# One transfer for the w_in rows of heads six and seven, and s and b issued from ScalarE's queue, in a fused gated-attention and squared-ReLU kernel

## The chip, the cores and the metric

The kernel runs on one core of a Trainium2 chip. The metric is the device time of one execution in microseconds (us). Three executions of the kernel before gave 203.92, 203.97 and 204.05 us, with a median of 203.97 us. The profiled execution took 204.18 us.

## The reference

The program computes a gated linear attention for every batch and head, lays the heads side by side, and sends each token through a two-layer network with a squared ReLU:

```python
batch, n_heads, seq, head_dim = (4, 8, 768, 48)
n_tokens, d_model, d_ff = (3072, 384, 2048)

for t in range(S):
    state = alpha[:, :, t, :, None] * state + np.einsum('bhd,bhe->bhde', k[:, :, t], v[:, :, t])
    y[:, :, t] = np.einsum('bhd,bhde->bhe', q[:, :, t], state)

x = np.ascontiguousarray(attn_out.transpose(0, 2, 1, 3)).reshape(B * S, H * D)
h = x @ w_in
r = np.maximum(h, 0.0)
g = s * (r * r) + b
return (g @ w_out).astype(np.float32)
```

All inputs and the output are float32; `s` and `b` are one number each.

## The kernel before

The 3072 tokens are cut into 24 blocks of 128, six for each batch entry. Block n goes through these helpers, each named here with its engine and its line:

- `load` (L135) issues four DMAs from SyncE's queue: alpha, k, q and v of the block, each 192 KB in pieces of 192 bytes. Eight buffers of each exist.
- `ln` (L202, ScalarE) takes the logarithm of alpha; `cum` (L217 and L220, TensorE) sums it along the block, and ScalarE turns the sums into the decay factors at L228, L229 and L231.
- `qk` (L245 and L246, VectorE) scales k and q, `tr` (L251, TensorE, copied out by VectorE at L256) transposes them, `amat` (L266, masked at L274) makes the 128 by 128 score blocks.
- `vcast` (L206 and L210, GpSimd) casts v to bf16. Heads 0 to 5 go to `vp_sb` and heads 6 and 7 to `vz_sb`. The 48 columns of a head stand at places 0, 1, 2 of groups of four, and every fourth place is left for a part of head 6 or 7. So the eight heads of 48 fill three tiles of 128 rows, and `w_in` has to be loaded with its rows in the matching order.
- `inter` and `yp` (L282, L301, L326) make the attention output, which ScalarE copies to `xd_all` at L334; `state` (L345 to L366) carries the state on, mostly on GpSimd.
- `mm1` (L382) multiplies by `w_in`, ScalarE applies the ReLU (L390), VectorE squares (L397), and `mm2` (L411) multiplies by `w_out`.

The weights come in once. `load_w_in` (L142) is called for each half of the 2048 columns. Of each half, three transfers (L145) bring the rows of heads 0 to 5, 384 KB each to 32 partitions, and two (L148) bring the rows of heads 6 and 7, 192 KB each to 16 partitions. Every piece is 4 KB long. The weights are cast to bf16 by `cast_w_in` (L157 on ScalarE, L159 on VectorE), called `win` in the order below. `w_out` comes in four transfers and is scaled by `s` as it is cast (L163 and L171); `b` is used once, when `bias_row` makes the bias (L188).

The order of every engine is written out by hand; the framework only adds the semaphore waits. SyncE issues load(0), load(1), the two halves of `w_in`, `s`, `b`, load(2), load(3), the four parts of `w_out` and load(4) to load(7), in this order, before the blocks begin. ScalarE starts with a table load (L434). Its next instruction is `ln(0)`. The opening of the blocks is this list; `busy` (L192) are multiplications whose result nobody reads, and an engine runs its own part of the list in order:

```python
(ln, 0), (vcast, 0), (cum, 0), (qk, 0), (busy, 7), (tr, 0),
(ln, 1), (vcast, 1), (busy, 4), (cum, 1), (amat, 0), (qk, 1), (busy, 5),
(y, 0), (tr, 1), (busy, 4), (amat, 1), (busy, 6), (y, 1), (win, 0), (win, 1), (busy, 3),
(m, 0, 0), (m, 1, 0), (m, 0, 1), (m, 1, 1), (busy, 7), (win, 2), (win, 3), (ln, 2), (m, 0, 2), (cum, 2),
```

In the trace, every DMA of this kernel adds to one of eight completion semaphores. They are taken in turn in program order: the first DMA adds to the first semaphore, the ninth to the first again. From the ninth on, a DMA waits, before it is issued, until the one that used the same semaphore eight places earlier is complete.

Of the kernel before, what the change touches and what calls it, by code (L numbers as in the profile page):

```python
# [19 lines left out]
def kernel(  # L20
# [12 lines left out]
    nc = tc.nc  # L33
# [9 lines left out]
    KT = d_model // 128  # L43
# [32 lines left out]
    s_col = sb.tile([128, 1], FP32, name="s_col")  # L76
    b_col = sb.tile([128, 1], FP32, name="b_col")
# [30 lines left out]
    w_in_st = sb.tile([128, KT, d_ff], FP32, name="w_in_st")  # L108
# [14 lines left out]
    def load_a(n, eng=None):  # L123
        (eng or nc.sync).dma_start(out=al_sb[n % NLD], in_=src(alpha, n))

    def load_q(n, eng=None):
        (eng or nc.sync).dma_start(out=q_sb[n % NLD], in_=src(q, n))

    def load_k(n, eng=None):
        (eng or nc.sync).dma_start(out=k_sb[n % NLD], in_=src(k, n))  # L130

    def load_v(n, eng=None):
        (eng or nc.sync).dma_start(out=v_sb[n % NLD], in_=src(v, n))  # L133

    def load(n):  # L135
        if n < NBLK:
            load_a(n)
            load_k(n)
            load_q(n)
            load_v(n)  # L140

    def load_w_in(c0, c1):  # L142
        six = moe_w_in[0 : 96 * KT, c0:c1].rearrange("(t a b) f -> b a t f", t=KT, b=3)
        for r in range(3):
            nc.sync.dma_start(out=w_in_st[r::4, :, c0:c1], in_=six[r])  # L145
        two = moe_w_in[96 * KT :, c0:c1].rearrange("(x t a) f -> x a t f", x=2, t=KT)
        for e in range(2):
            nc.sync.dma_start(out=w_in_st[64 * e + 3 : 64 * e + 64 : 4, :, c0:c1], in_=two[e])  # L148

    def load_w_out(j0, j1):  # L150
        nc.sync.dma_start(
# [52 lines left out]
    def vcast(n):  # L204
        vs = v_sb[n % NLD]
        nc.gpsimd.tensor_copy(  # L206
            out=vp_sb[n % 3].rearrange("s h (a b) -> s h a b", b=4)[:, :, :, 0:3],
            in_=vs[:, 0:6].rearrange("s h (a b) -> s h a b", b=3),
        )
        nc.gpsimd.tensor_copy(  # L210
            out=vz_sb[n % 3].rearrange("s e t (a b) -> s e t a b", b=4)[:, :, :, :, 3],
            in_=vs[:, 6:8].rearrange("s e (t a) -> s e t a", t=3),
        )

    def cum(n):
# [218 lines left out]
    nc.scalar.preload_act_table_set("natural_log_exp_and_others")  # L434
    load(0)
    load(1)
    quarter = d_ff // 4
    load_w_in(0, 2 * quarter)
    load_w_in(2 * quarter, d_ff)
    nc.sync.dma_start(out=s_col, in_=moe_s.to_broadcast((128, 1)))  # L440
    nc.sync.dma_start(out=b_col, in_=moe_b.to_broadcast((128, 1)))
    load(2)
    load(3)
    for j in range(0, NJ, 4):
# [43 lines left out]
    for pos, what in enumerate(  # L488
# [5 lines that stand above are left out]
            (qk, 2), (m, 1, 2), (vcast, 2), (mm1, 0, 3), (tr, 2), (sq, 0, 3), (mm1, 1, 3), (ln, 3), (amat, 2), (sq, 1, 3),  # L494
            (busy, 4), (cum, 3), (busy, 3), (qk, 3), (y, 2), (vcast, 3), (busy, 2), (tr, 3), (m, 2, 0), (mm1, 2, 1),
            (amat, 3), (mm1, 2, 2), (wout, 0), (mm1, 2, 3), (sq, 2, 1), (sq, 2, 2), (sq, 2, 3), (busy, 2), (y, 3),
            (wout, 1), (o, 0, 0), (o, 1, 0), (m, 3, 0), (m, 3, 1), (wout, 2), (o, 0, 1), (o, 1, 1), (colsum, 1), (m, 3, 2),
            (m, 3, 3), (o, 2, 0), (wout, 3), (o, 2, 1), (ln, 4), (cum, 4), (colsum, 2), (o, 0, 2), (vcast, 4), (o, 1, 2), (o, 2, 2),
            (colsum, 3), (qk, 4), (o, 1, 3), (o, 2, 3), (tr, 4), (colsum, 4), (o, 0, 3), (amat, 4),
        ]  # L500
    ):
        at(0.1 * pos, *what)
# [12 lines left out]
    for n in range(4, NBLK):  # L515
        p = 8 * n
        if n > 4:
            f = min((n - 5) / 3.0, 1.0)
            c, t, a = 7.0 + 7.8 * f, 4.8 + 6.0 * f, 2.2 + 5.7 * f
# [44 lines left out]
```

## Time and profile before

| What | Value |
|---|---|
| Median of three executions | 203.97 us |
| Profiled execution | 204.18 us |
| Its span, first to last instruction | 202.4 us |
| Granted TensorE clock | 1.00 |
| TensorE matmul busy | 190.0 us (94%) |
| VectorE, ScalarE, GpSimd busy | 149.9, 105.8, 74.5 us |
| TensorE busy from 76 to 190 us | 113.71 of 114 us |
| TensorE busy from 24 to 76 us | 49.05 of 52 us |
| TensorE busy from 0 to 4 us | 0 |
| `busy` multiplications (L192) | 44, 13.57 us, none after 76 us |
| DMA read and written | 25.19 and 4.74 MB |
| DMA busy share by tenths, 0 to 70 us | 9 or more in nearly every slice after the first |

The share of an engine's busy time is an average over an opening of some 76 us, in which engines wait for one another, and a steady part in which TensorE never rests. The instructions of a queue start in order, and a DMA's row in the timeline begins when its waits are over. The landing of a DMA is the time at which its semaphore has all sixteen counts; the trace has these times too. For the first eight DMAs (alpha, k, q, v of blocks 0 and 1) they are 3.74, 5.11, 6.16, 7.19, 8.26, 9.32, 10.37 and 11.15 us, and for the five of the first half of `w_in` 12.29, 14.09, 16.01, 16.62 and 17.59 us.

### The profile page before, as it was taken

What the parts mean: (1) busy time and instruction counts of PE and PEld (TensorE: products, weight loads), DVE (VectorE), ACT (ScalarE), POOL (GpSimd) and SP (SyncE); (2) the same over time, 40 slices, a digit from 0 to 9 for tenths busy, and PEclk for the clock granted to TensorE, in tenths of its full rate; (3) what the DMA queues carried; (4) which work ended last, traced back from release to release, by engine and by line L of the source; (5) the groups of instructions that cost most, each with busy time, mean ns of one, the idle gap of its engine ahead of it and who ended that gap; (6) DMA issues with size and microseconds to landing.
All of it is one profiled execution on the core that took longest, in us unless ns stands there. A gap on an engine that the chain in (4) does not pass through costs nothing.

```text
span 202.4 us, 6402 instructions
## 1 busy us (share of the span) xinstructions
PE 190.0 (94%) x2580; PEld 147.1 (73%) x2583; DVE 149.9 (74%) x289; ACT 105.8 (52%) x210; POOL 74.5 (37%) x171
## 2 busy tenths in 40 slices
PE   1999989999989899999999999999999999999993
PEld 1455768675766787888788788878887878888871
DVE  6366687778789689999976877877876887796341
ACT  3224865383376565554655655565465555544440
POOL 8344015421530066447440524632600662362000
PEclk9999999999999999999999999999999999999999
DMA  6999999999999927958596957955996691111102
GB/s 123 197 283 325 175 193 355 300 175 188 172 189 172 134 27 134 160 126 189 104 241 127 193 118 126 198 100 98 173 215 110 97 198 40 43 39 42 40 3 78
DMA packets 112924, 30.35 MB, mean 150 GB/s; under 512 B 106991, under 2 KB 112126, under 8 KB 112894
## 3 DMA queue, kind: packets, MB, share of 16 engines
q1 hardware_dynamic: 112894, 29.94, 76.1%
q8 instruction: 20, 0.33, 0.7%
q14 instruction: 10, 0.08, 0.2%
HBM read 25.19 MB, written 4.74 MB: 148 GB/s over the span
## 4 chain that ended last, share of the span: by engine, by line
PE 75%; DVE 8%; DMA 5%; SPq 5%; ACT 3%; issue 2%; DVEq 0%; ACTq 0%
PE h_ps L382 28%; PE o_ps L411 25%; PE ct_ps L251 5%; PE y_ps L301 5%; DMA w_in_st<-in_moe_w_in_dram 3%; PE a_ps L266 3%; PE y_ps L282 3%; ACT r_sb L390 2%; PE a_ps L411 2%; PE h_ps L192 2%; DMA q_sb<-in_q_dram 2%; PE ct_ps L217 2%; DVE gt_all L397 1%; DVE qb_sb L246 1%; SPq L133 1%
## 5 line engine op out<-in xcount | busy, mean ns | idle before, releaser
L390 ACT ACTIVATE r_sb<-h_ps 128x512 bf16<-128x512 f32 x96 | 57.3, 599 | 52.0 <-PE h_ps L382 51.5
L382 PE MATMUL h_ps<-xd_all,w_in_bf 128*128 128x128 bf16 x1152 | 79.0, 219 | 0.6 <-ACT w_in_bf L157 0.3
L382 PEld LDWEIGHTS <-w_in_bf 128*128 128x128 bf16 x1152 | 70.7, 98 | 9.8 <-ACT w_in_bf L157 0.8
L397 DVE TENSOR_TENSOR gt_all<-r_sb 128x512 bf16<-128x512 bf16 x96 | 48.4, 508 | 32.5 <-ACT r_sb L390 32.3
L411 PE MATMUL o_ps<-w_out_bf,gt_all 128*128 128x384 bf16 x336 | 68.4, 327 | 0.3 <-DVE out_sb L424 0.3
L353 POOL TENSOR_TENSOR sd_sb<-t_sb,blast 48x144 bf16<-48x144 f32 x40 | 18.0, 451 | 93.8 <-DVE t_sb L347 52.8
L411 PEld LDWEIGHTS <-gt_all 128*128 128x128 bf16 x384 | 33.1, 98 | 16.4 <-issue 0.3
L228 ACT ACTIVATE bi_sb<-ct_ps 128x384 f32<-128x384 f32 x24 | 11.8, 491 | 17.6 <-PE ct_ps L217 13.7
L206 POOL CAST vp_sb<-v_sb 128x288 bf16<-128x288 f32 x24 | 14.6, 610 | 15.8 <-DMA v_sb<-in_v_dram 15.7
L256 DVE COPY qkT<-ct_ps 112x1024 bf16<-112x1024 bf16 x24 | 16.5, 688 | 5.3 <-PE ct_ps L251 5.3
L334 ACT ACTIVATE xd_all<-y_ps 128x384 bf16<-128x384 f32 x24 | 11.8, 490 | 13.0 <-PE y_ps L301 12.9
L274 DVE TENSOR_TENSOR am_a<-a_ps,mask 128x512 bf16<-128x512 f32 x24 | 16.4, 683 | 1.8 <-PE a_ps L266 1.6
L246 DVE TENSOR_TENSOR qb_sb<-q_sb,b_sb 128x384 bf16<-128x384 f32 x24 | 16.3, 678 | 0.7 <-ACT b_sb L229 0.7
L245 DVE TENSOR_TENSOR kb_sb<-k_sb,bi_sb 128x384 bf16<-128x384 f32 x24 | 13.4, 560 | 4.4 <-ACT bi_sb L228 4.4
L274 DVE TENSOR_TENSOR am_b<-a_ps,mask 128x512 bf16<-128x512 f32 x24 | 16.3, 679 | 0.0
L202 ACT ACTIVATE la_sb<-al_sb 128x384 bf16<-128x384 f32 x24 | 12.4, 515 | 4.0 <-DMA al_sb<-in_alpha_dram 4.0
L192 PE MATMUL h_ps<-mask,U_bf 128*128 128x512 bf16 x44 | 13.6, 422 | 0.8 <-ACT r_sb L390 0.6
L359 POOL TENSOR_TENSOR sd_sb<-t_sb,blast 48x48 bf16<-48x48 f32 x40 | 14.2, 354 | 0.0
L251 PEld LDWEIGHTS <-qb_sb 128*112 128x112 bf16 x96 | 8.8, 133 | 5.6 <-DVE qb_sb L246 3.3
L210 POOL CAST vz_sb<-v_sb 128x96 bf16<-128x96 f32 x24 | 12.2, 509 | 0.0
L217 PE MATMUL ct_ps<-la_sb,U_bf 128*128 128x384 bf16 x24 | 8.0, 333 | 4.4 <-ACT la_sb L202 4.4
L229 ACT ACTIVATE b_sb<-ct_ps 128x384 f32<-128x384 f32 x24 | 11.7, 486 | 0.7 <-DMA row_dr<-b_sb 0.7
(64 smaller groups left out, 202.9 us busy)
## 6 DMA issues: line engine op xcount, KB each, us to landing
al_sb<-in_alpha_dram SPq DMA_DIRECT2D x24, 192.0 KB, 3.1
k_sb<-in_k_dram SPq DMA_DIRECT2D x24, 192.0 KB, 3.7
q_sb<-in_q_dram SPq DMA_DIRECT2D x24, 192.0 KB, 5.1
v_sb<-in_v_dram SPq DMA_DIRECT2D x24, 192.0 KB, 4.8
out_dram<-out_sb SPq DMA_DIRECT2D x19, 192.0 KB, 1.9
w_out_st<-in_moe_w_out_dram SPq DMA_DIRECT2D x4, 768.0 KB
w_in_st<-in_moe_w_in_dram SPq DMA_DIRECT2D x6, 384.0 KB, 6.6
out_dram<-keep_sb SPq DMA_DIRECT2D x5, 192.0 KB
```

Source lines behind the costliest of these rows:

```text
L192: nc.tensor.matmul(out=h_ps[i % 2], lhsT=U_bf, rhs=mask4.rearrange("a p t -> a (p t)"), start=True, stop=True,)
L206: nc.gpsimd.tensor_copy(out=vp_sb[n % 3].rearrange("s h (a b) -> s h a b", b=4)[:, :, :, 0:3], in_=vs[:, 0:6].rearrange("s h (a b) -> s h ...
L246: nc.vector.tensor_tensor(out=qb_sb[n % 2][:, :, 0:48], in0=q_sb[n % NLD], in1=b_sb[n % 2], op=ALU.mult)
L251: nc.tensor.transpose(out=t_ps[0:112, x, p, :], in_=t.rearrange("a h d -> a (h d)")[:, 128 * p : 128 * p + 112], identity=ident,)
L256: nc.vector.tensor_copy(out=qkT_sb[n % 2][0:112].rearrange("a x p t -> a (x p t)"), in_=t_ps[0:112].rearrange("a x p t -> a (x p t)"),)
L274: nc.vector.tensor_tensor(out=am_sb[e][n % 2], in0=a_ps[e], in1=mask4, op=ALU.mult)
L353: nc.gpsimd.tensor_tensor(out=cols[:, 0:3, :, 0:3], in0=t1_sb[r, 0:3].rearrange("k p (a b) -> k p a b", b=3), in1=bl[r, 0:3].unsqueeze(3). ...
L359: nc.gpsimd.tensor_tensor(out=cols[:, 3:6, :, 3], in0=t1_sb[r, 3].rearrange("k (t a) -> k t a", t=3), in1=bl[r, 3:4].to_broadcast([48, 3, ...
L382: nc.tensor.matmul(out=hp[:, jj * N : (jj + 1) * N], lhsT=w_in_bf[:, kk, 128 * j : 128 * (j + 1)], rhs=xd_sb[g][:, kk, 0:N], start=(kk == ...
L390: nc.scalar.activation(out=rs, in_=hp, func=AF.Relu)
L397: nc.vector.tensor_tensor(out=gt_sb[g][:, u * 512 : (u + 1) * 512], in0=rs, in1=rs, op=ALU.mult)
L411: nc.tensor.matmul(out=op[:, 0:d_model], lhsT=gt_sb[g][:, j * N + t * C : j * N + (t + 1) * C], rhs=w_out_bf[:, j, :], start=(j == 0), sto ...
```

## The change

Three edits. The rows of `w_in` for heads 6 and 7 go to the partitions in another order, so that one transfer to 32 partitions replaces two to 16, once for each half. The cast of v for these heads reads its source in the matching order, with a step of three elements instead of one. And the two DMAs of `s` and `b` are issued from ScalarE's queue, after load(1) and before `w_in` in program order, instead of from SyncE's queue after `w_in`.

```diff
@@ load_w_in
-        two = moe_w_in[96 * KT :, c0:c1].rearrange("(x t a) f -> x a t f", x=2, t=KT)
-        for e in range(2):
-            nc.sync.dma_start(out=w_in_st[64 * e + 3 : 64 * e + 64 : 4, :, c0:c1], in_=two[e])
+        two = moe_w_in[96 * KT :, c0:c1].rearrange("(i t) f -> i t f", t=KT)
+        nc.sync.dma_start(out=w_in_st[3::4, :, c0:c1], in_=two)
@@ vcast
             out=vz_sb[n % 3].rearrange("s e t (a b) -> s e t a b", b=4)[:, :, :, :, 3],
-            in_=vs[:, 6:8].rearrange("s e (t a) -> s e t a", t=3),
+            in_=vs[:, 6:8].rearrange("s e (a t) -> s e t a", t=3),
@@ the opening
     nc.scalar.preload_act_table_set("natural_log_exp_and_others")
     load(0)
     load(1)
+    nc.scalar.dma_start(out=s_col, in_=moe_s.to_broadcast((128, 1)))
+    nc.scalar.dma_start(out=b_col, in_=moe_b.to_broadcast((128, 1)))
     quarter = d_ff // 4
     load_w_in(0, 2 * quarter)
     load_w_in(2 * quarter, d_ff)
-    nc.sync.dma_start(out=s_col, in_=moe_s.to_broadcast((128, 1)))
-    nc.sync.dma_start(out=b_col, in_=moe_b.to_broadcast((128, 1)))
     load(2)
     load(3)
```

## The prediction

> **What bounds the kernel now.** I read the busy slices first, then the list of waits of TensorE, then the timelines of ScalarE, TensorE and SyncE's queue in the opening.
>
> ```profile
> PE   1999989999989899999999999999999999999993
> PEclk9999999999999999999999999999999999999999
> DMA  6999999999999927958596957955996691111102
> ...
> PE ct_ps L217 <- ACT la_sb L202: 4.4, 1, 4.4
> PE ct_ps L251 <- DVE qb_sb L246: 1.7, 4, 0.7
> ...
> 0.73 1.28 ACT L434 ACT_TABLE_LOAD   x1 [0.73 <-PEq L548]
> 3.83 0.52 ACT L202 ACTIVATE la_sb<-al_sb 128x384 bf16<-128x384 f32 x1 [1.82 <-DMA al_sb<-in_alpha_dram]
> ...
> 5.03 3.15 PE L192 MATMUL h_ps<-mask,U_bf 128*128 128x512 bf16 x7
> 7.97 0.63 PE L251 MATMUL ct_ps<-ident,qb_sb 128*112 128x128 bf16 x4
> ...
> 17.23 0.49 ACT L334 ACTIVATE xd_all<-y_ps 128x384 bf16<-128x384 f32 x1 [4.05 <-PE y_ps L301]
> 17.70 1.15 ACT L157 ACTIVATE w_in_bf<-w_in_st 128x512 bf16<-128x512 f32 x2
> ...
> 22.47 1.15 ACT L157 ACTIVATE w_in_bf<-w_in_st 128x512 bf16<-128x512 f32 x2 [0.16 <-DMA w_in_st<-in_moe_w_in_dram]
> ...
> SPq L440 <- DMA w_in_st<-in_moe_w_in_dram: 1.3, 1, 1.3
> ...
> 9.44 0.60 SPq L145
> ...
> 16.03 0.53 SPq L440 DMA_DIRECT2D s_col<-in_moe_s_dram  x1
> ```
>
> TensorE is full from the second slice at the full clock. Its only long wait is the first (the columns are the sum, how often, and the longest): 4.4 us until ln(0) has run on ScalarE, itself idle from 2.01 (0.73 + 1.28) to 3.83 us, until alpha of block 0 has landed. In TensorE's order cum(0) stands ahead of everything else, and seven fillers and tr(0) follow at once (5.03, 7.97). So the path that sets the end starts at ln(0), and whatever delays ln(0) delays all of TensorE's program, unless a later wait has slack to take it up.
>
> The DMA slices look as full, so I checked whether data is late anywhere. The chain that ended last names w_in, landed at 17.59, as what released the casts at 17.7. But ScalarE's cast starts at 17.70, the end of its copy of y(1) (17.23 + 0.49 = 17.72): at once, with no idle time. The second half's cast waited 0.16 us for data, and TensorE does not wait for that cast (fillers run to 23.81). Of the blocks, alpha(2) lands at 23.27 for use at 23.53, q(2) at 25.61 for 26.01; the four w_out parts land at 33.35, 36.28, 38.38, 40.83 and their casts begin at 35.38, 37.81, 40.71, 43.83. So the loads are close, but none is last.
>
> The SyncE row matters most. The issue of s (L440) at 16.03 waited for a w_in transfer whose data it does not touch. The third w_in transfer, issued at 9.44, landed at 16.01 by the trace's completion counts. It is the 11th DMA and s is the 19th: the turn of eight semaphores. Likewise b started at 16.64 after the 12th landed (16.62), alpha(2) at 17.61 after the 13th (17.59), k(2) at 18.32 after the 14th (18.31).
>
> **The change part by part.**
>
> **s and b on ScalarE.** All eight semaphores are already taken in turn by SyncE's DMAs alone, so a DMA from ScalarE has none of its own. Exactly eight DMAs stand ahead of s in the new order. So s becomes the ninth and must wait for the first, alpha(0), and b the tenth, which must wait for the second, k(0). Both waits stand on ScalarE's queue ahead of ln(0). What is queued behind them is ln(0), and TensorE, then VectorE, wait for that.
>
> Duration of an issue: no DMA is issued by ScalarE in this trace. The nearest rows are these two DMAs on SyncE, 0.528 us (L440) and 0.567 us (L441), which I take. From below: 0.303 us, the shortest L239 issue. From above: 1.251 us, the longest of the first eight loads (L133 at 2.65), if two queues hinder each other.
>
> The sum: alpha(0) is complete at 3.74, and 0.05 later (the gap the SyncE rows show) s is issued, 3.79 to 4.32. k(0) was issued at 1.23; its median of 3.7 us to landing gives 4.93, its own completion count 5.11, which I take. b is issued from 5.16 to 5.73, and ln(0) starts at 5.78 instead of 3.83: **1.95 us late**. With the short issue b ends at 5.46 and ln(0) is 1.7 us late. With the long one s ends at 5.04, b at 6.41, and it is 2.6 us late. No end is below zero, since the b wait alone ends 1.3 us after ln(0)'s present start.
>
> What is late next: cum(0), the seven fillers, tr(0), and so on, by the same 1.95 us, since none of TensorE's later waits in its list names a DMA. VectorE's casts and ScalarE's ReLUs are released by TensorE and move along. The slack that could take some of it up is ScalarE's 0.16 us at 22.47, which TensorE does not see. I subtract nothing.
>
> **SyncE's queue loses four DMAs.** Per half one w_in issue goes, 0.64 us (10.08 to 10.72), so the second half starts 0.64 us sooner. s and b go with their waits (14.67 to 17.20). alpha(2) becomes the 19th DMA and waits for the 11th, now the first w_in transfer (12.29), so it can go at about 13.4 instead of 17.61, k(2) at 14.1 instead of 18.32. The engines that move the data are full, so the landings gain far less than the issues. The gain is **nothing** on the path: the loads are not last now, and less so if the compute comes 1.95 us later. The new waits for s and b on SyncE (the 17th and 18th DMAs, reached at 12.0 and 12.7) are over: even with the 6.7 us that s took from issue to landing behind w_in, s lands at 10.5 and b, with 6.4, at 11.6.
>
> **One w_in transfer for two.** Same bytes, same 4 KB pieces, 32 partitions like L145. The pair of the first half added 1.58 us to the landings (16.01 to 17.59), the two L145 transfers before it 1.80 (14.09 less 12.29) and 1.92 (16.01 less 14.09), for 384 KB each. So the merged one costs between 0.34 us more and, at the best half rate of the pair (0.61 for 192 KB), 0.36 less. I take 0.1 more; it is covered, since the casts would be wanted near 19.65 (17.70 + 1.95) and not before. Without that cover, 0.1 would be on the path.
>
> The Trainium skill's "SBUF — State Buffer", section "Door 1: The DMA port swizzle", holds that a transfer to partitions of one half of the memory reaches only half of the ports; the pair was of that kind. By that rule the merged transfer would be about twice as fast, by an estimate some 0.8 us off the landing (half of the pair's 1.58); the landings above show the pair no slower than its neighbours, so the trace does not bear it out, and the sum with it would still be +1.95.
>
> **vcast's source order.** The vz cast (L210) takes 0.402 us in the median, with a contiguous source. A step of three is in no GpSimd row. From below: unchanged. From above: 1.126 us, the longest L210 here, so 0.7 us more. I take 0.1. y(3) has the least cover: its cast ends at 34.89 and its vz weights load at 36.91, 2.0 us later. From 76 us on vcast is placed well over a block ahead. **Nothing** at either bound; with the cover gone it would be 0.1 us per block, 2.4 in all.
>
> **The sum** against the profiled execution (span 202.4, with what lies around it 204.18): 204.18 + 1.95 = 206.13 us. That execution stood 0.21 above the median of the runs, so in terms of the median 203.97 + 1.95 = **205.9 us**.
>
> **The rivals.**
>
> *A: ScalarE does not wait.* If its two DMAs take a semaphore that nobody holds, they fit between 2.01 and 3.83: two issues of 0.57 with gaps end at 3.25. Then ln(0) stays, and nothing else is on the path: 203.9 us, no change. For it: the trace has no DMA from ScalarE. Against: a 1.3 us wait of just this kind at L440. The Trainium skill's "DMA: Bandwidth & Descriptors", section "Issuing engines are not separate DMA queues", says that issuing from a second engine saves the sequencer's time for the issue and nothing else; by that rule alone this case would hold. The trace shows that an issue also carries a wait, which the rule leaves out.
>
> *B: faster, because w_in and the loads really set the opening.* Place: the casts at 17.7 and 22.47. Price: the 0.16 us of ScalarE and TensorE's waits for the casts (0.30, and 0.27 for its weight load), 0.7 us in all: 203.3 us. It decides only if ScalarE holds ln(0) by less than that. For it: the chain puts 3% on w_in. Against: the copy of y(1) ends when the cast starts.
>
> *C: the delay is partly taken up.* If the two largest waits of TensorE in the opening that I read as compute, 0.71 us ahead of L251 at 66.31 and 0.38 us ahead of L301 at 59.35, hide late data instead, they do not move along, and 1.09 us is won back: 204.8 us. Against: both name VectorE, which is behind TensorE's own results there.
>
> *D: dearer.* The two issues run into the longest SyncE ones and k(0) lands later, pushed back by the 4-byte pieces: over 2.7 us, 207 us.
>
> **How the numbers follow.** Forecast 0.72, C 0.10, A 0.09, B 0.05, D 0.04. The forecast's own range, from the issue bounds, is 205.6 to 206.6. C belongs into the range, and A and B (0.14) stay out, with the outer edges of D: 204.4 to 206.9. Measurement of this kernel cannot tell less than about 0.2% (0.4 us) from no change. Slower by more than that: forecast, C and D, 0.86. Within it: A, 0.09. Faster: B, 0.05.
>
> **What would show it.** Right: in ScalarE's timeline two DMA issues between 3.8 and 5.8, the second waiting for k_sb, and ln(0) near 5.8; TensorE's first wait near 6.4 instead of 4.4; the first w_in cast near 19.7 with no wait for w_in; from 76 us on the same distances as now. SyncE issues alpha(2) near 13.4. Wrong: ScalarE's issues ahead of 3.3 (A); ln(0) late but the casts near 17.7 (C, and then the list of waits must show what took it up); the vz cast last ahead of L301 in the steady part, which would be a cost that I put at nothing.

## The result: slower by a quarter of the forecast delay

| | Before | After |
|---|---|---|
| Median (22 executions each, same chip) | 204.0 us | 204.5 us |
| Lowest and highest | 203.38, 204.85 us | 203.96, 205.0 us |
| Profiled execution | 204.18 us | 204.5 us |
| Its span | 202.4 us | 202.7 us |

The ratio is 1.0023 with an interval of 1.0012 to 1.0033, or +0.47 us (0.24 to 0.67). The forecast was +1.95 us. The sign was right by luck: the cause named for it was not there, and what did cost time had no term in the sum.

ScalarE's timeline of the changed kernel in the opening (start, duration, engine, line, operation, and in brackets the idle time before it and what ended that):

```profile
0.73 1.28 ACT L433 ACT_TABLE_LOAD   x1 [0.73 <-PEq L547]
0.76 0.56 ACTq L436 DMA_DIRECT2D s_col<-in_moe_s_dram  x1
1.35 0.61 ACTq L437 DMA_DIRECT2D b_col<-in_moe_b_dram  x1
4.23 0.52 ACT L201 ACTIVATE la_sb<-al_sb 128x384 bf16<-128x384 f32 x1 [2.21 <-DMA al_sb<-in_alpha_dram]
...
17.87 0.49 ACT L333 ACTIVATE xd_all<-y_ps 128x384 bf16<-128x384 f32 x1 [4.30 <-PE y_ps L300]
18.26 1.14 ACT L156 ACTIVATE w_in_bf<-w_in_st 128x512 bf16<-128x512 f32 x2
```

Both issues run at 0.76 and 1.35 us, inside the table load (0.73 to 2.01). Neither waits, and ScalarE sits idle for 2.21 us after them. What keeps ln(0) until 4.23 us, 0.40 later than before, is alpha itself: by the completion counts alpha(0) lands at 4.14 us instead of 3.74. TensorE's first wait, in its list of waits, grows by the same amount, from 4.4 to 4.8 us:

```profile
PE ct_ps L216 <- ACT la_sb L201: 4.8, 1, 4.8
```

Why alpha lands later can be seen in the view of the DMA engines for the first 8 us, in slices of 0.2 us (busy tenths, then GB/s). First the changed kernel, then the kernel before:

```profile
DMA  0000000004669985588977212369999999999999
GB/s 0 0 0 0 0 0 0 0 0 67 110 127 245 185 124 105 95 124 180 207 149 116 41 12 41 56 122 250 248 260 257 254 207 199 181 204 205 175 175 173
```

```profile
DMA  0000000002589999979999999799999999999999
GB/s 0 0 0 0 0 0 0 0 0 51 100 160 259 259 241 216 183 161 200 210 230 241 226 187 140 122 210 204 209 201 223 205 182 195 190 175 181 202 206 192
```

Before, the engines are full from 2.4 us on, but for two slices at 7 tenths. After, two holes open: 95 to 124 GB/s from 2.8 to 3.6 us, and 12 to 56 GB/s from 4.4 to 5.2. The pieces of s and b run from 2.52 to 5.43 us, so both holes lie inside their time. The page shows what these DMAs are: 288 packets of next to no bytes on a queue of their own (q10).

```profile
q10 hardware_dynamic: 288, 0.00, 0.1%
```

Everything behind them is late: k(0) lands at 6.30 us instead of 5.11, q(0) at 7.36 (6.16), v(0) at 8.41 (7.19), alpha(1) at 9.45 (8.26), v(1) at 12.20 (11.15). The last transfer of the first half of w_in is nevertheless complete at 17.22 us, where before it was 17.59: from v(1) to there it takes 5.01 us instead of 6.44.

How far ScalarE's instructions stand behind those of before, taken by pairing the two timelines:

| Stretch | Later than before by |
|---|---|
| 3.8 to 13 us | 0.40 us (ln(1), behind the late alpha(1), 1.19) |
| 17 us (copy of y(1)) | 0.64 us |
| 20 to 26 us | 0.38 us (the cast of the second half 0.12) |
| 28 to 48 us | 0.68 us |
| 49 to 58 us | 0.46 us |
| 60 to 76 us | 0.61 us |
| 78 us to the end | 0.27 us |

The 0.64 at 17 us comes from VectorE: its two scalings of k(1) and q(1) take 0.68 and 0.66 us instead of 0.55 each, since vcast(1), which waits for the later v(1), now runs on GpSimd at the same time. In the thirteen profiles in which vcast(1) has ended before them, each of the two takes 0.55 to 0.56 us. The last step down to 0.27 is a wait of TensorE before that is gone after; its line in the list of waits of before has no counterpart in that of after:

```profile
PE o_ps L411 <- DVE out_sb L424: 0.3, 1, 0.3
```

These two executions differ by 0.32 us, and the medians by 0.5.

### The profile page after: what moved, and what is told of

Read it like the earlier page. It is cut to its first block, busy times and chain, and to the rows that moved or that the text cites. A ratio compares the mean times of both kernels' runs of the same rounds, so it can differ in the third digit from the quotient of the medians.

```text
span 202.7 us, 6398 instructions
## 1 busy us (share of the span) xinstructions
PE 189.9 (94%) x2580; PEld 146.9 (72%) x2583; DVE 150.5 (74%) x289; ACT 105.4 (52%) x210; POOL 75.1 (37%) x171
## 4 chain that ended last, share of the span: by engine, by line
PE 66%; SPq 23%; DMA 4%; DVE 3%; issue 1%; ACT 0%; ACTq 0%
PE o_ps L410 24%; PE h_ps L381 24%; SPq L130 7%; SPq L127 6%; PE y_ps L300 4%; PE ct_ps L250 4%; SPq L124 4%; SPq L133 3%; PE a_ps L265 3%; PE y_ps L281 2%; DMA k_sb<-in_k_dram 2%; SPq L145 2%; DMA q_sb<-in_q_dram 2%; SPq L150 2%; PE a_ps L410 1%
## 5 line engine op out<-in xcount | busy, mean ns | idle before, releaser
L396 DVE TENSOR_TENSOR gt_all<-r_sb 128x512 bf16<-128x512 bf16 x96 | 48.9, 513 | 32.4 <-ACT r_sb L389 32.3
L352 POOL TENSOR_TENSOR sd_sb<-t_sb,blast 48x144 bf16<-48x144 f32 x40 | 19.0, 474 | 98.2 <-DVE t_sb L346 61.7
L227 ACT ACTIVATE bi_sb<-ct_ps 128x384 f32<-128x384 f32 x24 | 11.8, 490 | 16.5 <-PE ct_ps L216 13.4
L333 ACT ACTIVATE xd_all<-y_ps 128x384 bf16<-128x384 f32 x24 | 11.7, 490 | 13.4 <-PE y_ps L300 13.3
L245 DVE TENSOR_TENSOR qb_sb<-q_sb,b_sb 128x384 bf16<-128x384 f32 x24 | 16.9, 703 | 0.5 <-DMA q_sb<-in_q_dram 0.5
L358 POOL TENSOR_TENSOR sd_sb<-t_sb,blast 48x48 bf16<-48x48 f32 x40 | 13.3, 331 | 0.0
L250 PE MATMUL ct_ps<-ident,qb_sb 128*112 128x128 bf16 x96 | 9.7, 225 | 2.1 <-DVE qb_sb L245 1.3
```

The lines of the kernel that those rows point to most:

```text
L245: nc.vector.tensor_tensor(out=qb_sb[n % 2][:, :, 0:48], in0=q_sb[n % NLD], in1=b_sb[n % 2], op=ALU.mult)
L250: nc.tensor.transpose(out=t_ps[0:112, x, p, :], in_=t.rearrange("a h d -> a (h d)")[:, 128 * p : 128 * p + 112], identity=ident,)
L352: nc.gpsimd.tensor_tensor(out=cols[:, 0:3, :, 0:3], in0=t1_sb[r, 0:3].rearrange("k p (a b) -> k p a b", b=3), in1=bl[r, 0:3].unsqueeze(3). ...
L396: nc.vector.tensor_tensor(out=gt_sb[g][:, u * 512 : (u + 1) * 512], in0=rs, in1=rs, op=ALU.mult)
```

## The experiments

The theory after the result: the 4-byte pieces of s and b cost the loads of block 0 some 0.4 us on alpha and 1.2 us on the rest, the first delay goes through to the end, and the merged w_in transfer gives part of it back. Rivals: a second queue as such is what disturbs; the merge does nothing; ln(0) does not pass its delay on. Each ratio is to the kernel before on the same chip, with its 95% interval. Edits are to the kernel before unless another is named. "The merge" is the first two hunks of the change (the rows of w_in and the source of the vz cast).

### Only s and b moved

```diff
     load(1)
+    nc.scalar.dma_start(out=s_col, in_=moe_s.to_broadcast((128, 1)))
+    nc.scalar.dma_start(out=b_col, in_=moe_b.to_broadcast((128, 1)))
...
-    nc.sync.dma_start(out=s_col, in_=moe_s.to_broadcast((128, 1)))
-    nc.sync.dma_start(out=b_col, in_=moe_b.to_broadcast((128, 1)))
```

> Only s and b move to ScalarE's queue; w_in and the vz cast stay as before. Theory (the 4-byte pieces of s and b, moved by a second queue beside load(0), hold up alpha(0)): ln(0) starts near 4.2 instead of 3.83 and the time is 0.3 to 0.6 us above before, like the whole change. Rival (the merged w_in transfer or the new cast order is what costs): ln(0) late or not, the time is within 0.15 us of before.

Measured 1.0051 (1.0031 to 1.0071). alpha(0) lands at 4.18 us, k(0) at 6.03, the first half of w_in at 18.25, 0.66 later than before. ScalarE's timeline:

```profile
4.27 0.52 ACT L202 ACTIVATE la_sb<-al_sb 128x384 bf16<-128x384 f32 x1 [2.26 <-DMA al_sb<-in_alpha_dram]
...
17.91 0.49 ACT L334 ACTIVATE xd_all<-y_ps 128x384 bf16<-128x384 f32 x1 [4.05 <-PE y_ps L301]
18.36 1.15 ACT L157 ACTIVATE w_in_bf<-w_in_st 128x512 bf16<-128x512 f32 x2
```

ln(0) is as late as in the whole change, so this part alone is enough to make the loss. The ratio is +1.0 us, more than the 0.3 to 0.6 expected. Here the late w_in holds the first cast as well (18.25 landed, 18.36 cast), but only 0.06 us longer than the copy does, so the rest stays open.

### Only the merge

Its edit is the change's first two hunks; s and b stay behind w_in on SyncE.

> Only the merged w_in transfer and the vz order; s and b stay on SyncE behind w_in. Theory: ln(0) at 3.83, GpSimd's vz cast at 0.40 us in the median as before, time within 0.2 us of before. Rival (merge or cast order costs): 0.3 to 0.6 us above before with ln(0) at 3.83.

Measured 0.9985 (0.9969 to 1.0001). ScalarE's timeline:

```profile
3.88 0.52 ACT L201 ACTIVATE la_sb<-al_sb 128x384 bf16<-128x384 f32 x1 [1.87 <-DMA al_sb<-in_alpha_dram]
...
16.95 0.49 ACT L333 ACTIVATE xd_all<-y_ps 128x384 bf16<-128x384 f32 x1 [4.05 <-PE y_ps L300]
17.34 1.14 ACT L156 ACTIVATE w_in_bf<-w_in_st 128x512 bf16<-128x512 f32 x2
```

The first half is complete at 16.29 us, 1.3 earlier than before. The cast follows the copy of y(1) by 0.39 us and waits for nothing. The earlier landing is clear. GpSimd's vz cast stands at 0.59 us in the median instead of the expected 0.40, and nobody waits for it. A gain in time is likely but not shown, since the interval just includes none: most of what the merge saves on the landing is not needed.

### s and b early, but from SyncE

```diff
     load(1)
+    nc.sync.dma_start(out=s_col, in_=moe_s.to_broadcast((128, 1)))
+    nc.sync.dma_start(out=b_col, in_=moe_b.to_broadcast((128, 1)))
```

The merge stays, and the later pair of SyncE issues goes.

> As the change, but s and b are issued by SyncE at the same written place, after load(1). Theory (two queues beside each other cost, the pieces alone do not): ln(0) at 3.83, the landing of w_in's first transfer comes no more than 0.3 us later for the pieces ahead of it, time within 0.2 us of before. Rival (4-byte pieces hold the DMA engines for 1.2 us wherever they stand): ln(0) at 3.83 too, but w_in's first half lands about 1.2 us later than 17.6 and the first cast starts near 18.8: 0.8 to 1.2 us above before.

Measured 1.0012 (0.9995 to 1.0028). Behind v(1), which lands at 10.98 us, s lands at 11.14, b only at 12.61 and the first w_in transfer at 13.56. The first half is complete at 17.93, 1.6 us later than with the merge alone, and the cast waits for it although the copy of y(1) began at 17.23:

```profile
17.23 0.49 ACT L333 ACTIVATE xd_all<-y_ps 128x384 bf16<-128x384 f32 x1 [4.06 <-PE y_ps L300]
18.03 1.15 ACT L156 ACTIVATE w_in_bf<-w_in_st 128x512 bf16<-128x512 f32 x2 [0.31 <-DMA w_in_st<-in_moe_w_in_dram]
```

So the pieces cost more than 1 us on SyncE's queue too. It is not ScalarE's queue that is dear. The time, +0.2 us with an interval that includes none, is less than the rival's 0.8 to 1.2: the merge had made the landing earlier, and the first cast is only 0.33 us later than before.

### s and b from ScalarE, but behind ln(1)

```diff
+    def sb_load():
+        nc.scalar.dma_start(out=s_col, in_=moe_s.to_broadcast((128, 1)))
+        nc.scalar.dma_start(out=b_col, in_=moe_b.to_broadcast((128, 1)))
...
-            (ln, 1), (vcast, 1), (busy, 4), (cum, 1), (amat, 0), (qk, 1), (busy, 5),
+            (ln, 1), (sb_load,), (vcast, 1), (busy, 4), (cum, 1), (amat, 0), (qk, 1), (busy, 5),
```

With the merge. Run twice.

> As the change, but ScalarE issues s and b behind ln(1), in the middle of the loads. Theory (two queues cost about 1.2 us of DMA time wherever they meet): ln(0) at 3.83; while the pieces of s and b run, the 192-byte pieces or w_in fall behind by about 1.2 us, w_in's first half lands near 18.5 and the first cast waits for it, 0.5 to 0.8 us above before. Rival (only the first loads are hurt, because there the engines start up): no dip, time within 0.2 us of before. Where ScalarE has to wait for a turn of the semaphores it shows in the start of the two issues.

> The change with s and b issued by ScalarE behind ln(1), a second time, beside the changed kernel on the same chip. Theory: 0.996 to 0.9985 of before, and below the changed kernel by 0.3% or more. Rival (its first result was luck with the start of the clock): within 0.1% of before.

Measured 0.9972 (0.9956 to 0.9987), and 0.9992 (0.9976 to 1.0008) the second time. ScalarE's timeline of the first:

```profile
3.89 0.52 ACT L201 ACTIVATE la_sb<-al_sb 128x384 bf16<-128x384 f32 x1 [1.88 <-DMA al_sb<-in_alpha_dram]
8.08 0.52 ACT L201 ACTIVATE la_sb<-al_sb 128x384 bf16<-128x384 f32 x1 [1.89 <-DMA al_sb<-in_alpha_dram]
8.09 0.55 ACTq L472 DMA_DIRECT2D s_col<-in_moe_s_dram  x1
8.68 0.81 ACTq L473 DMA_DIRECT2D b_col<-in_moe_b_dram  x1
...
17.13 1.14 ACT L156 ACTIVATE w_in_bf<-w_in_st 128x512 bf16<-128x512 f32 x2
```

The pieces now run from 11.05 to 13.84 us, beside the 4 KB pieces of w_in, whose first half is complete at 16.50 (16.37 in the second), about as early as without them (16.29 with the merge alone). In both runs ln(0) and the first cast (17.13, 17.52) come ahead of those of the changed kernel. The first time lies below what either expected, and the second run took back most of that lead.

### Only s early

```diff
     load(1)
+    nc.scalar.dma_start(out=s_col, in_=moe_s.to_broadcast((128, 1)))
...
-    nc.sync.dma_start(out=s_col, in_=moe_s.to_broadcast((128, 1)))
     nc.sync.dma_start(out=b_col, in_=moe_b.to_broadcast((128, 1)))
```

> On the kernel before, only s is issued by ScalarE at the start; b stays with SyncE. Theory (cost by the piece): about half of the delay, k(0) lands near 5.7 (5.11 before, 6.30 with both), alpha(0) no later than 4.14. Rival (cost of using a second queue at all): alpha(0) at 4.14 and k(0) at 6.3 as with both.

Measured 1.0031 (1.0017 to 1.0045). ln(0) at 4.26 us, as late as with both; but k(0) lands at 5.14 and v(1) at 11.33, much as before. Neither expectation fits: s by itself makes the first delay (0.43 us on alpha(0)) and none of the second. That suggests that of the two holes in the DMA row the first belongs to s and the second to b.

### One extra 4-byte DMA from ScalarE

```diff
     load(1)
+    nc.scalar.dma_start(out=one_sb[0:1], in_=moe_s.to_broadcast((1, 1)))
```

> On the kernel before, ScalarE issues one extra DMA of a single 4-byte piece at the start; nothing reads it. s and b stay with SyncE. Theory (cost by the piece): alpha(0) and k(0) land within 0.1 us of 3.74 and 5.11, time within 0.1 us of before. Rival (cost of a second queue at all, or of two issues at the same moment): alpha(0) near 4.1 again, time 0.2 to 0.5 us above.

Measured 0.9974 (0.9957 to 0.9991), with alpha(0) at 3.65 us, k(0) at 4.77 and v(1) at 10.49. The issue by ScalarE as such costs nothing. What two queues do beside each other this run does not show: its one piece is through at 1.65 us, before the first piece of the loads starts at 1.85. That the loads of both blocks were complete earlier than in any other run, and the time with them, is not explained; the instruction adds work and removes none.

### ScalarE held up

```diff
+    for _ in range(14):
+        nc.scalar.activation(out=scr_sb, in_=U_bf, func=AF.Copy)
+
     events = []
```

> On the kernel before, ScalarE runs 14 copies that nobody reads before ln(0), so that ln(0) starts late with no DMA changed. By the prediction's step that every delay of ln(0) reaches the end: end and ln(0) shift by the same amount within 0.3 us (at some 0.25 us a copy ln(0) starts near 5.5, 1.7 us late, and the time is 205.6). Rival (slack in the opening takes it up): the end shifts by half of ln(0)'s delay or less.

Measured 1.0117 (1.0079 to 1.0154), which is +2.4 us (1.6 to 3.1, from four executions); the profiled execution took 206.78 us, 2.60 more than that of before. ScalarE's timeline:

```profile
2.02 4.74 ACT L467 ACTIVATE scr_sb<-U_bf 128x128 bf16<-128x128 bf16 x14
6.67 0.51 ACT L203 ACTIVATE la_sb<-al_sb 128x384 bf16<-128x384 f32 x1
```

ln(0) is 2.84 us late, and 0.8 to 0.9 of that arrives at the end (2.4 by the ratio, 2.60 by the profiled executions). So a delay of the size that the prediction had in mind would have cost most of what it said.

### q(0) and v(0) from ScalarE's queue

```diff
-    load(0)
+    load_a(0)
+    load_k(0)
+    load_q(0, nc.scalar)
+    load_v(0, nc.scalar)
```

> On the kernel before, q(0) and v(0), with their usual 192-byte pieces, are issued by ScalarE instead of SyncE, so that two queues run beside each other with no 4-byte piece. Theory A (changing between queues costs the engines time): the last of the four loads of block 0 lands about 1 us later than 7.19. Theory B (it is the 4-byte pieces beside the other queue): the four are complete by 7.2, only in another order, alpha(0) and k(0) later because q and v share the engines with them.

Measured 1.0023 (1.0005 to 1.0042). alpha(0) lands at 4.50 us, since q(0) now shares the engines with it, and ln(0) comes at 4.58. Block 0 is complete at 7.13 (7.19 before). So two queues do not slow down the sum of the transfers; they divide it otherwise, and the first load pays. The profiled execution (204.19 us) was no longer than that of before although its ln(0) was 0.75 late, and the ratio over ten executions shows a loss: one execution alone doesn't carry a verdict here.

### Extra pieces from 128 addresses, short and long

```diff
     load(1)
+    nc.scalar.dma_start(out=d0_sb, in_=q[3, 7, 0:128, 0:1])
+    nc.scalar.dma_start(out=d1_sb, in_=q[3, 7, 128:256, 0:1])
```

The first kernel adds two DMAs of 128 pieces of 4 bytes, each piece from an address of its own. The second takes whole rows of 48 numbers (192 bytes) instead.

> On the kernel before, ScalarE issues two extra DMAs at the start, each of 128 pieces of 4 bytes like s and b, but from 128 addresses 192 bytes apart instead of one address. s and b stay with SyncE. Theory A (a 4-byte piece costs, wherever it reads): alpha(0) near 4.15, k(0) near 6.1, v(1) near 12 (11.15 before), like s and b. Theory B (128 reads of one address cost): alpha(0) within 0.1 us of 3.74, v(1) within 0.3 of 11.15.

> As the last, but the two extra DMAs have 128 pieces of 192 bytes each, 24 KB each and an eighth of a load. Theory A (short pieces cost): alpha(0) and k(0) later by no more than the data's share, 0.13 us each (a load takes 1.05 us of stream), v(1) within 0.3 us of 11.15. Theory B (any DMA beside the first loads costs by its pieces): alpha(0) near 4.15 and v(1) near 12 again.

Measured 0.9996 (0.9981 to 1.0011) and 1.0016 (1.0003 to 1.0029). With the short pieces alpha(0) lands at 3.85 us, k(0) at 5.09, v(1) at 11.12; with the long ones at 4.00, 5.19 and 11.38. The long ones delay alpha(0) by 0.26 us, twice the data's share that was expected. As many pieces of the same 4 bytes from the same queue at the same time cost a tenth of a microsecond or nothing where those of s and b cost 0.4 and 1.2. What is left as the difference is that s and b read one address 128 times, in small tensors of their own. The short run also shows what the kernel before hid, in ScalarE's timeline:

```profile
16.88 0.49 ACT L336 ACTIVATE xd_all<-y_ps 128x384 bf16<-128x384 f32 x1 [4.16 <-PE y_ps L303]
17.71 1.15 ACT L159 ACTIVATE w_in_bf<-w_in_st 128x512 bf16<-128x512 f32 x2 [0.34 <-DMA w_in_st<-in_moe_w_in_dram]
```

Here the copy is early, the half lands at 17.61 us, and the cast starts 0.10 later, at the time of the kernel before. With this landing, as with that of the kernel before (17.59), the cast cannot start ahead of 17.7 us. That landing scatters: in six other runs without the merge it came at 16.36 to 17.52.

### s and b late, without the merge

The edit of the run behind ln(1), with the w_in transfers of before.

> The kernel before with s and b issued by ScalarE behind ln(1), and w_in and the vz order as before. Against the run with the merge and the same late issue (0.9972 of before) it shows the merge alone. Theory (the merge brings the first half of w_in about 1 us sooner, and that is worth some 0.3 us): w_in's first half lands near 17.4, time 0.9985 to 1.001 of before. Rival (the merge does nothing, the late issue is what helps): 0.997, w_in's first half near 16.5.

Measured 1.0006 (0.9993 to 1.0019), the time of the theory; the landing lies between the two expected. The half is complete at 16.81 us, 5.82 after v(1); with the merge these were 5.48 and 5.39. Beside the two runs with the merge (0.9972 and 0.9992) that makes 0.1 to 0.3% for it, in line with the merge alone; the intervals of 1.0006 and 0.9992 overlap.

### s and b ahead of the first cast

```diff
-            (y, 0), (tr, 1), (busy, 4), (amat, 1), (busy, 6), (y, 1), (win, 0), (win, 1), (busy, 3),
+            (y, 0), (tr, 1), (busy, 4), (amat, 1), (busy, 6), (y, 1), (sb_load,), (win, 0), (win, 1), (busy, 3),
```

With the merge and the helper `sb_load` from above.

> The change with s and b issued by ScalarE still later, ahead of the first w_in casts, so that nothing of theirs lies beside the loads of blocks 0 and 1. Theory: ln(0) near 3.85, w_in's first half near 16.4, time 0.996 to 0.999 of before, no worse than with the issue behind ln(1). Rival (the two issues on ScalarE, 0.6 us each, hold up the casts, which come right behind them in its order): first cast 0.5 to 1.2 us later, 1.001 to 1.005 of before.

Measured 1.0036 (1.0023 to 1.0048), as the rival said. ScalarE's timeline:

```profile
17.67 0.49 ACT L333 ACTIVATE xd_all<-y_ps 128x384 bf16<-128x384 f32 x1 [4.05 <-PE y_ps L300]
17.68 0.55 ACTq L472 DMA_DIRECT2D s_col<-in_moe_s_dram  x1
18.26 0.61 ACTq L473 DMA_DIRECT2D b_col<-in_moe_b_dram  x1
19.05 1.15 ACT L156 ACTIVATE w_in_bf<-w_in_st 128x512 bf16<-128x512 f32 x2 [0.89 <-DMA w_in_st<-in_moe_w_in_dram]
```

The cast would follow the copy at 18.06 us (17.67 + 0.39, the distance in the run of the merge alone). It starts at 19.05, behind the second issue. The releaser in the brackets misleads: that half had landed at 15.81. An issue on ScalarE is free while ScalarE waits for data or loads a table, and the two cost nearly their full time (0.99 of 1.19 us) where ScalarE's next instruction sets the path.

This run also shows the wait that the prediction looked for, on the other queue. SyncE's waits:

```profile
SPq L130 <- DMA s_col<-in_moe_s_dram: 6.5, 1, 6.5
```

k(2) takes its turn on the semaphore of s, so SyncE cannot issue it until s is complete (21.71 us), and it goes at 21.73 instead of 16.30 with the merge alone. The pieces of s and b run from 19.40 to 21.57 us, and from 20.0 to 21.2 the last 192-byte pieces of alpha(2) beside them move at 5 to 17 GB/s. All this cost little: against the merge alone ScalarE is 1.71 us late at this cast (0.72 of it in the copy) and 1.80 at the end.

### The change with other addresses

```diff
     load(1)
+    nc.scalar.dma_start(out=s_col, in_=q[3, 7, 0:128, 0:1])
+    nc.scalar.dma_start(out=b_col, in_=q[3, 7, 128:256, 0:1])
```

The changed kernel, except that the two DMAs read 128 numbers of q, which stand in for s and b.

> The whole change, with one thing different: the two DMAs of ScalarE read 128 numbers from 128 places of q instead of one number 128 times, so that other numbers stand in for s and b. Theory (the 128 reads of one address are the whole loss): ln(0) near 3.9, k(0) near 5.1, w_in's first half near 16.5; 0.996 to 0.9995 of before, like the merge alone (0.9985). Rival (early DMAs from ScalarE cost as such): ln(0) near 4.2 or the time at 1.001 to 1.004 of before, like the change.

> The changed kernel itself, beside the other two on the same chip. Both theories: ln(0) near 4.23, 1.001 to 1.004 of before.

Measured 0.9984 (0.9969 to 1.0000) with the other addresses, and 1.0007 (0.9991 to 1.0023) for the change. ScalarE's timeline and the first 8 us of the DMA engines with the other addresses:

```profile
0.77 0.42 ACTq L436 DMA_DIRECT2D s_col<-in_q_dram  x1
1.22 0.60 ACTq L437 DMA_DIRECT2D b_col<-in_q_dram  x1
3.91 0.52 ACT L201 ACTIVATE la_sb<-al_sb 128x384 bf16<-128x384 f32 x1 [1.89 <-DMA al_sb<-in_alpha_dram]
```

```profile
DMA  0000000001599999999999999999999999999999
GB/s 0 0 0 0 0 0 0 0 0 39 89 165 205 243 248 236 195 170 175 197 221 210 201 211 212 202 195 190 181 183 195 176 179 190 180 187 184 194 193 177
```

Same queue, nearly the same times of issue, same number and size of pieces, and both holes are gone. alpha(0) lands at 3.82 us, k(0) at 5.10 and the half at 16.11. In the change run again they came at 4.13, 6.09 and 17.36. The time is then that of the merge alone (0.9984 beside 0.9985). Its interval still overlaps that of the change run again, so the cause rests on the landings. Over all profiles, ln(0) is at 4.21 to 4.27 us in the four with s beside the first loads (from ScalarE), and at 3.73 to 3.96 in ten others; apart from these stand the 192-byte pieces (4.09), q(0) and v(0) on ScalarE (4.58) and ScalarE held up (6.67).

Since the change itself gave 1.0023 and 1.0007 in two sets of runs, its cost is 0.1 to 0.5 us. Whether the version behind ln(1) truly beats the kernel before stays open: 0.9972 and 0.9992 point to a gain of 0.3% at most.

## Why the prediction was wrong in its main step

**"So s becomes the ninth and must wait for the first, alpha(0)" is the step that failed.** It counted the turn of the semaphores in the order in which the DMAs are written. The completion counts of the changed kernel show another order: s and b count on two semaphores that no earlier DMA uses. alpha(0)'s is used next by q(1), k(0)'s by v(1), and those of s and b by the first two w_in transfers. So s and b stand among the first eight, ahead of q(1) and v(1), though they are written behind them. A likely reason is that the framework deals the semaphores after it has put the issues of all engines into an order of its own, in which ScalarE's two come early since nothing is queued ahead of them. No run tests the reason, but others bear it out that the turn isn't the written one. Behind ln(1), s and b are written behind load(7), with over 40 DMAs ahead of them, and take the ninth and eleventh place of the turn; ahead of the first cast they take the twelfth and thirteenth, and there k(2) had to wait 6.5 us for s. Rival A, that ScalarE doesn't wait, was right about that and put the issues at 2.01 to 3.25 us; they ran even earlier, beside the table load.

**An issue's price** was well bounded: 0.56 and 0.61 us measured against the 0.53 and 0.57 taken. It lay off the path, which the prediction did not expect.

**The path was right.** A delay of ln(0) goes through to the end: 0.8 to 0.9 of the 2.84 us with ScalarE held up, 0.47 of 0.75 with q(0) and v(0) on ScalarE, 0.27 or more of 0.40 in the change. "I subtract nothing" was a little too strict, as the wait for out_sb took up some 0.3 of what had grown to 0.6.

**What made the delay was named under D only as an addition**, "pushed back by the 4-byte pieces". It was the whole of it: 0.40 us on alpha(0) instead of 1.95 from a wait. The trace of before had no row for that cost: there the pieces of s and b pass from 19.8 to 21.6 us, behind w_in on its queue, and the rate stays at 141 GB/s or more.

**SyncE's queue:** it was forecast that alpha(2) could go at about 13.4 us instead of 17.61. SyncE's timeline of the changed kernel:

```profile
14.61 0.59 SPq L124 DMA_DIRECT2D al_sb<-in_alpha_dram  x1
```

That is 3.0 us sooner, 1.2 short of the forecast, which is what the loads ahead had lost. That it gains nothing on the path agrees with the last stretch, where the change is later and not earlier.

**The merged transfer** was mis-sized: +0.1 us, with −0.36 as the lower bound. From v(1) to the complete half, the runs without the merge took 5.30 to 6.49 us (6.12 in the mean of nine), those with it 4.93 to 5.48 (5.17 in the mean of seven; the run with s and b between the two on SyncE, 6.94, is left out). So it saves about 0.9 us. The spacing that the prediction used shows it too: from the third L145 landing to the end of the half it is 0.95 to 1.00 us in all eight runs with the merge and 1.51 to 1.72 in all nine without, so the term should have been −0.6. What misled was the price taken for a transfer to 32 partitions: the 1.80 and 1.92 us of the L145 transfers in this one trace were near the top of 0.98 to 1.97 in sixteen profiles. The Trainium skill's "SBUF — State Buffer", section "Door 1: The DMA port swizzle", by which a transfer to one half of the partitions reaches half of the ports, gave an estimate of 0.8 us; the prediction set it aside because the pair's landings were spaced like their neighbours'. The runs agree with the page's direction, and with the size of the estimate within 0.2 us. That it is the ports is not shown: the merge also makes one transfer of two, and no run here looks at ports directly.

**Rival B** was half right. The first cast starts at the later of two times: the copy of y(1) plus 0.39, and the landing plus 0.10. This holds within 0.01 us in every run but the one with the issues ahead of the cast. Before, these were 17.62 and 17.69, so w_in did hold the cast, by 0.07 us. Reading "at once, with no idle time" as "not waiting for data" hid a tie: a floor so close below means that a faster path gains almost nothing until the floor is moved. In the change the merge moved the landing to 17.22 us, and the copy, at 17.87, sets the cast.

**The vz cast** with a step of three costs next to nothing: its shortest is 0.392 us (0.394 before), its mean 525 ns (509; over all runs 534 with the step and 521 without). The median went from 0.402 to 0.585, but with the contiguous source it also stood at 0.50 in other runs. Nobody waits for it in the changed kernel.

## What to carry to other kernels

A load that spreads one number over all partitions is 128 reads of one address. Here it cost nothing to be seen beside or behind the 4 KB pieces of w_in, and 0.4 to 1.2 us beside the first short loads, for which the critical path waits: put it with the long ones. An order read from the source, of semaphores as of anything that a framework deals, has to be checked in the trace of a kernel that has the new engine in it. Where two conditions on an instruction lie within 0.1 us, both are on the path. A move to an idle queue is free only as long as the engine behind it has nothing due.

## What the hardware showed unexpectedly

**128 reads of one address.** Beside 192-byte pieces, s and b cost 0.4 us on the first load and 1.2 on the following ones, and moved 1 KB for it; from 128 addresses 0.1 and less; beside 4 KB pieces none was seen. s alone delayed alpha(0) by 0.43 us and k(0) by none. That the one address is the cause rests on the runs with other addresses; how it slows the engines is not shown.

**TensorE's early pace varies from run to run.** The first `busy` multiplications start every 0.427 us, later ones every 0.216. The time of the switch differs widely between runs whose code up to there is the same. TensorE's timeline with s and b behind ln(1), with the merge and then without:

```profile
5.09 2.88 PE L191 MATMUL h_ps<-mask,U_bf 128*128 128x512 bf16 x7
...
8.26 1.03 PE L191 MATMUL h_ps<-mask,U_bf 128*128 128x512 bf16 x4
```

```profile
5.15 3.15 PE L192 MATMUL h_ps<-mask,U_bf 128*128 128x512 bf16 x7
...
8.94 1.85 PE L192 MATMUL h_ps<-mask,U_bf 128*128 128x512 bf16 x4
```

The same four multiplications take 1.03 and 1.85 us. The views give a granted clock of 1.00 from the start in both, but ahead of the switch that is no reading: the trace's first clock record, at full speed, starts at 7.57 us in the first run and at 10.60 in the second, 3.1 and 6.1 us after TensorE's first multiplication, and there the pace changes. So "at the full clock" in the prediction did not hold for the first 9 us. Over the seventeen profiles the copy of y(1) starts 12.85 to 14.01 us behind ln(0), nearly in the order of that switch. This is a likely part of the scatter from 203.4 to 204.9 us, and why one execution of a kernel can't tell 0.2%. The Trainium skill's "TensorE: Matmul & The Clock Gate", section "Part 1: The HAM clock gate (the "warmup" mystery)", describes such a start: half speed until a free-running window of 3.4 us has passed, and different from run to run. The pace agrees; the spread here is wider than the 0.5 us to either side that it states.
